# Tile stages in fewer bundles, memory sums with k and v side by side, final sums by pairs of experts, last weights in pieces

## The chip, the cores and the metric

The kernel runs on one core of one Trainium2 chip. The metric is the device time of one execution in microseconds (us); lower is better. The time before is the median of three runs.

## What is computed

Three layers in a row, cut from the reference; all data in fp32. x is first a memory attention over 4 batches of 576 tokens, then a mixture of 4 experts, then a soft mixture of 8 experts with 4 slots each.

```python
# attention: batch 4, heads 8, seq 576, head_dim 64, 32 memories
a = softmax(phi, over the sequence)
k_m = einsum('bhsm,bhsd->bhmd', a, k);  v_m = einsum('bhsm,bhsd->bhmd', a, v)
attn_out = softmax(q @ k_m.T / 8) @ v_m            # 2304 tokens x 512
# first mixture: 4 experts, D = 512, F = 1024
p = domain_probs / domain_probs.sum(-1)
out += p[:, e] * (relu(x @ w1[e]) @ w2[e])          # for e in 0..3
# second mixture: 8 experts, 4 slots each
logits = x @ phi2
slot_input = softmax(logits, over the tokens).T @ x
slot_out[e] = relu(slot_input[e] @ w1[e]) @ w2[e]   # v1, v2 in the kernel
out = softmax(logits, over the slots) @ slot_out
```

## The kernel before

The tokens run in five units: batches 0 to 2 whole (576 tokens), batch 3 as two halves of 288. The second mixture's input is never formed. `up` computes hidden values of the first mixture for 128 hidden units and up to 288 tokens: a **bundle** of six fp32r passes 128x288 (L767 to L769) over the attention weights A and the product g of w1 with v's memory (`g_mult`, L692, one w1 block of 1 MB each, copied out by ACT L701 and DVE L703). ACT takes the relu (L776), DVE transposes in 32x32 blocks (L782), POOL multiplies by p (L786); the result h stays for the slot sums. `logits` (L805, L812) multiplies the relu by M = w2 phi2, summed over hidden units in one PSUM bank.

M comes from `m_chunk`, eight chunks of 1 MB of w2: four whole-array transposes per chunk in four stages (**flips**, L836), copied by ACT or DVE (L842), then `part` (L854, 128x32 tiles, N = 128) and one more flip (L865). The batch's attention needs `memory`: flips `tops` (L465) and `back` (L480) for the maximum of phi, exp on ACT (L493), then the sums of k and v with the exp in four `whole` stages (L511, L516; 128x32 tiles, 64 columns), k first, v later; `total` (L530, L534) sums the exp; two flips `turn` (L554). `query` flips q (L600) and scores it (L612) five times a batch.

When a unit ends, `group` gathers its logits (L914, L919, L923) in a bank, ACT copies it to lr (L927), DVE transposes it to lc (L934), ACT takes the exp (L948), DVE transposes to dt (L954), and PE sums exp times h into four banks by `sums` (L972): 32x32 tiles, the row by the token block's quarter, the column by 2 x (block mod 2) + pair of experts. DVE adds them to srun (L992). After the last unit come the end stages: `turn_s` (L1201), w2 blocks (L1232), `slots` (L1246), v1 blocks (W1, L1275), flips (L1289), v2 blocks (W2, L1319) in 128x16 tiles, the fold of four tiles' rows into one (L1340), and the output (L1358), sent by SP and, for the last 64 tokens of each batch, by POOL (L365). `warm` (L1067) is a transpose of the identity that only keeps PE busy. R[0] to R[4] are places in SBUF; a weight block of the end goes to a place as soon as its last reader is through.

What sets the order: every stage is added with a due time `at`, a cost and keys that it reads and writes. `Plan.order` runs through time at build and gives each engine the ready stage with the smallest due time. For PE it keeps two classes: bundles (lag None) and all others. Among bundles another stage has to be due a LAG of 1 before the next bundle; outside, a bundle has to be due AHEAD of 8 before the others. TURN is the cost it puts on a change of class. `Uses` then settles which PSUM bank and SBUF place each use gets. m_at, a table of numbers, and base + offsets in `attention` set the due times.

```python
            gap = stages[a][0] - stages[b][0]
            return b if gap >= (stages[b][8] if tokens else -self.AHEAD) else a
```

Of the kernel before, what the change touches and what calls it, by code (L numbers as in the profile page):

```python
# [14 lines left out]
class Plan:  # L15
# [7 lines left out]

    HOP = 0.1
    RATE = 0.33
    LAG, AHEAD = 1, 8
# [40 lines left out]
    def order(self):  # L67
# [16 lines left out]
        def first(cand, t):  # L84
            cand = [n for n in cand if ready[n] <= t]
            a = min((n for n in cand if stages[n][8] is None), default=None)
            b = min((n for n in cand if stages[n][8] is not None), default=None)
            if a is None or b is None:
                return b if a is None else a
            gap = stages[a][0] - stages[b][0]  # L90
            return b if gap >= (stages[b][8] if tokens else -self.AHEAD) else a
        out = []
        while len(out) < len(stages):
# [57 lines left out]
class Uses:  # L151
# [7 lines left out]
    def __call__(self, *places, width=1):  # L159
        uid = len(self.kinds)  # L160
        self.kinds.append((places, width))
        return Use(self.found[uid] if self.found else places[0], uid)

    def settle(self, stages):
# [169 lines left out]
def program(  # L334
# [107 lines left out]
    def memory(b, at):  # L442
# [25 lines left out]
        add(PE, 0.4, tops, r=[("ph", 2), ("ph", 3), mxk, "cst"], w=[pk(b1)], at=at[1])  # L468
# [12 lines left out]
        add(PE, 0.4, back, r=[mbk, "cst"], w=[pk(b2)], at=at[2])  # L481
# [23 lines left out]
        def whole(w, c, t):  # L505
            rows = slice(64 * c, 64 * c + 64)
            for r_ in range(5):
                for i in range(4):
                    o = t[32 * i:32 * i + 32, 0:64]
# [11 lines left out]
        b3, b4 = att_bank(b), att_bank(b)  # L521
        for c, bk in enumerate((b3, b4)):
            add(PE, 0.85, lambda c=c, bk=bk: whole(0, c, bank[bk]),
                r=[("ph", c), ("ph", 2 + c), ("kt", 0, c), wk(o + 1024 * c, 1024)], w=[pk(bk)], at=at[4])
        t3 = bank[b4][:, 128:256]
# [9 lines left out]
        add(PE, 0.9, total, r=[smk, ("ph", 2), ("ph", 3), "cst"], w=[pk(b4)], at=at[4] + 0.1)  # L535
# [6 lines left out]
        def scaled(bks, dst, eng):  # L542
            for c in range(2):
                src = bank[bks[c]][:, 0:64]
# [20 lines left out]
        add(PE, 0.25, lambda: turned(km, kd, bank[b5], PE), r=[kmk, "cst"], w=[pk(b5)], at=at[5] + 0.1)  # L565
        add(DVE, 0.5, lambda: turned(km, kd, bank[b5], DVE), r=[pk(b5), "cst"], w=[("kb", b % 2)],
            at=at[5] + 0.2)
        b6 = [att_bank(b), att_bank(b)]
        for c in range(2):
            add(PE, 0.85, lambda c=c: whole(1, c, bank[b6[c]]),  # L570
                r=[("ph", c), ("ph", 2 + c), ("kt", 1, c), wk(o + 2048 + 1024 * c, 1024)], w=[pk(b6[c])],
                at=at[6])
        add(ACT, 0.65, lambda: scaled(b6, vm, ACT), r=[pk(b6[0]), pk(b6[1]), "rs"], w=[vmk], at=at[7])
        b7 = att_bank(b)
        add(PE, 0.25, lambda: turned(vm, vd, bank[b7], PE), r=[vmk, "cst"], w=[pk(b7)], at=at[8])
# [13 lines left out]
    def query(b, ti, at):  # L589
# [11 lines left out]
        add(PE, 0.42, flip, r=[qk, "cst"], w=[pk(b1)], at=at[0])  # L601
# [14 lines left out]
        add(PE, 0.5, score, r=[wk(qo, 512), ("kb", b % 2)], w=[pk(b2)], at=at[1])  # L616
# [62 lines left out]
    def g_mult(s, at):  # L679
# [7 lines left out]
        bs = [g_bank(), g_bank()]  # L687
# [61 lines left out]
    def up(u, n, fb, ki):  # L749
# [20 lines left out]
        add(PE, 0.81, f, r=[wk(go, 2048)] + a_part(b, 0, o0, w) + a_part(b, 1, o0, w), w=[pk(bm)], at=at, lag=None)  # L770
# [19 lines left out]
    def logits(u, n, at):  # L790
# [7 lines left out]
        def f():  # L798
# [11 lines left out]
            else:  # L810
                for m, ho in enumerate(hos):
                    nc.tensor.matmul(  # L812
                        lb[32 * (m % 4):32 * (m % 4) + 32, 0:HB], M[:, 4 * n0 + m, :], at_place(ho, HB),
# [3 lines left out]
        add(PE, 1.1, f,  # L817
            r=[("M", m) for m in range(n0, n + 1)] + [wk(o, width) for o in hos], w=[pk(LB)], at=at, lag=0)


    def m_chunk(n, ats):
# [9 lines left out]
        for a in range(4):  # L831
            bk = g_bank()
# [6 lines left out]
            add(PE, 0.42, flip, r=[wk(o + 512 * a, 512), "cst"], w=[pk(bk)], at=ats[1 + a])  # L839
# [9 lines left out]
        bk = g_bank()  # L849
# [583 lines left out]
```

## Time and profile before

| what | us |
|---|---|
| median of three runs (499.54 to 500.55) | 500.46 |
| the profiled execution | 503.48 |
| its span | 501.7 |
| PE busy | 472.7 |
| DVE busy | 297.4 |
| POOL busy | 214.7 |
| ACT busy | 199.7 |

Each matmul of fp32 appears as two passes in the trace, transposes and the fp32r bundles as one. Starts of passes lie closer together than they last, since passes overlap: the distance of two starts is what one costs, not its duration. The granted clock is the share of TensorE's 2.4 GHz that the chip gives in a stretch; 0.50 is 1.2 GHz. Idle time of an engine stands in brackets with what ended it.

### The profile page before, as it was taken

Reading aid. Unit: us, or ns where it says so; the run is one execution under the profiler, and the core shown is the slowest. Engines: PE = TensorE matmul, PEld = TensorE weight load, DVE = VectorE, ACT = ScalarE, POOL = GpSimd, SP = SyncE. Lnnn points to the kernel's source line nnn. Section 1 sums busy time; section 2 is a strip of 40 time slices with the busy share of each in tenths; the row PEclk is TensorE's granted clock in tenths of the full one; section 3 lists DMA queues with packets and bytes.
Section 4 is the critical chain, followed back from the end, with each engine's and each line's share of the span. In section 5 each row is a group of like instructions: output and inputs, shape, how many; then the busy total and the mean of one; then the engine's idle time right before and its main releaser. Section 6 shows DMA issues by size and latency. Waiting matters only on the chain.

```text
span 501.7 us, 13501 instructions
## 1 busy us (share of the span) xinstructions
PE 472.7 (94%) x5732; PEld 340.7 (68%) x5732; DVE 297.4 (59%) x606; ACT 199.7 (40%) x476; POOL 214.7 (43%) x259
## 2 busy tenths in 40 slices
PE   4899799999999999999999999999999989999991
PEld 2677688778876888788668887865797866333330
DVE  6589447676695867767684676676677544110041
ACT  2354245555551556555145555533552420011031
POOL 0244134557641448775224778533765940000001
PEclk9999899999999999999999999999999998789996
DMA  7999867425320946352082645524536997999928
GB/s 220 220 353 309 331 181 220 170 59 178 144 86 11 338 121 162 109 188 85 3 276 81 203 169 175 204 86 149 157 133 227 370 341 302 421 421 422 421 111 305
DMA packets 65404, 106.09 MB, mean 211 GB/s; under 512 B 28608, under 2 KB 40896, under 8 KB 59712
## 3 DMA queue, kind: packets, MB, share of 16 engines
q1 hardware_dynamic: 65152, 104.71, 61.3%
q8 instruction: 45, 0.74, 0.6%
q0 software_dynamic: 192, 0.52, 0.4%
q14 instruction: 15, 0.12, 0.1%
HBM read 100.50 MB, written 4.72 MB: 210 GB/s over the span
## 4 chain that ended last, share of the span: by engine, by line
PE 88%; DMA 4%; SPq 3%; DVE 1%; ACT 1%; issue 0%; DVEq 0%; ACTq 0%
PE ps L767 15%; PE ps L769 13%; PE ps L768 13%; PE ps L972 8%; PE ps L692 6%; PE ps L805 5%; PE ps L1275 4%; PE ps L836 3%; PE ps L1319 3%; SPq L365 3%; DMA raw<-in_moe_w_dram 3%; PE ps L1232 2%; PE ps L812 2%; DMA h<-in_moe_w_dram 2%; PE ps L854 2%; PE ps L600 2%
## 5 line engine op out<-in xcount | busy, mean ns | idle before, releaser
L786 POOL TENSOR_TENSOR h<-h,pe 128x576 f32<-128x576 f32 (+1 forms) x160 | 158.1, 996 | 137.6 <-DVE h L782 108.7
L767 PE MATMUL ps<-A,g 128*128 128x288 f32 x512 | 157.5, 308 | 0.0
L776 ACT ACTIVATE hts<-ps 128x288 f32<-128x288 f32 x256 | 105.2, 412 | 129.5 <-PE ps L769 128.1
L769 PE MATMUL ps<-A,g 128*128 128x288 f32 x512 | 151.5, 296 | 0.2 <-DVE g L703 0.2
L768 PE MATMUL ps<-A,g 128*128 128x288 f32 x512 | 151.2, 295 | 0.0
L782 DVE STREAM_TRANSPOSE h<-hts 128x576 f32<-128x576 f32 (+1 forms) x160 | 102.8, 648 | 46.9 <-ACT hts L776 46.5
L767 PEld LDWEIGHTS ps<-A,g 128*128 128x128 f32 x512 | 96.4, 188 | 21.5 <-issue 14.0
L769 PEld LDWEIGHTS ps<-A,g 128*128 128x128 f32 x512 | 96.2, 188 | 0.9 <-DVE g L703 0.9
L768 PEld LDWEIGHTS ps<-A,g 128*128 128x128 f32 x512 | 96.3, 188 | 0.1
L703 DVE TENSOR_TENSOR g<-ps,g 128x512 fp32r<-128x512 f32 x64 | 41.1, 680 | 17.8 <-ACT g L701 17.8
L701 ACT CAST g<-ps 128x512 fp32r<-128x512 f32 x64 | 34.9, 590 | 33.2 <-PE ps L692 33.2
L972 PE MATMUL ps<-h,dts 32*32 32x512 f32 x1152 | 40.0, 597 | 1.6 <-DVE dts L954 1.6
L365 POOL DMA_DIRECT2D out_dram<-v x4 | 2.3, 568 | 81.5 <-ACT v L1367 81.5
L692 PE MATMUL ps<-raw,vbs 64*32 64x512 f32 x512 | 35.2, 600 | 1.0 <-DMA raw<-in_moe_w_dram 1.0
L972 PEld LDWEIGHTS ps<-h,dts 32*32 32x32 f32 x1152 | 22.8, 103 | 15.2 <-issue 4.7
L805 PE MATMUL ps<-hts,M 128*32 128x288 f32 x384 | 28.2, 411 | 0.0
L629 POOL TENSOR_TENSOR atts<-atts,small 128x256 f32<-128x256 f32 (+1 forms) x20 | 11.5, 573 | 24.4 <-DVE small L627 24.3
L836 PE MATMUL ps<-ident,h 128*128 128x128 f32 x128 | 18.8, 286 | 2.8 <-DMA h<-in_moe_w_dram 2.8
L836 PEld LDWEIGHTS ps<-ident,h 128*128 128x128 f32 x128 | 15.1, 146 | 5.0 <-issue 3.6
L805 PEld LDWEIGHTS ps<-hts,M 128*32 128x32 f32 x384 | 10.4, 109 | 10.0 <-issue 4.5
L640 POOL TENSOR_TENSOR atts<-atts,small 128x256 f32<-128x256 f32 (+1 forms) x20 | 11.5, 573 | 13.4 <-DVE small L638 7.0
L842 DVE COPY h<-ps 128x512 f32<-128x512 f32 x16 | 10.8, 676 | 9.1 <-PE ps L836 9.0
(186 smaller groups left out, 519.7 us busy)
## 6 DMA issues: line engine op xcount, KB each, us to landing
raw<-in_moe_w_dram SPq DMA_DIRECT2D x32, 1024.0 KB, 5.2
v<-in_moe_w_dram SPq DMA_DIRECT2D x20, 1024.0 KB, 9.9
h<-in_moe_w_dram SPq DMA_DIRECT2D x18, 1024.0 KB, 9.0
h<-in_k_dram SPq DMA_DIRECT2D x8, 512.0 KB, 5.0
h<-in_v_dram SPq DMA_DIRECT2D x8, 512.0 KB, 6.5
atts<-in_moe_w_dram SPq DMA_DIRECT2D x4, 1024.0 KB, 8.1
atts<-in_q_dram SPq DMA_DIRECT2D x12, 256.0 KB, 5.8
atts<-in_phi_dram SPq DMA_DIRECT2D x8, 256.0 KB, 4.3
```

Of the source, the lines that this page charges most:

```text
L692: nc.tensor.matmul(bank[bs[c]][32 * i:32 * i + 32, :], vb[b % 2][64 * c:64 * c + 64, 32 * i:32 * i + 32], t()[64 * c:64 * c + 64, i, :], s ...
L701: add(ACT, act(512), lambda c=c, src=src: nc.scalar.copy(out=placed(g()[:, 2 * c]), in_=src), r=[pk(bs[c])], w=[wk(o + 1024 * c, 512)], at ...
L703: add(DVE, dve(512), lambda c=c, src=src: nc.vector.tensor_tensor(out=placed(g()[:, 2 * c + 1]), in0=src, in1=placed(g()[:, 2 * c].bitcast ...
L767: nc.tensor.matmul(t, gh, ah, start=(c == 0), stop=False)
L768: nc.tensor.matmul(t, gh, al, start=False, stop=False)
L769: nc.tensor.matmul(t, gl, ah, start=False, stop=(c == 1))
L776: add(ACT, act(w), lambda: nc.scalar.activation(out=t[:, o0 - base:o1 - base], in_=bank[bm][:, 0:w], func=ACTF.Relu,), r=[pk(bm)], w=[wk(h ...
L782: add(DVE, dve(width), lambda: nc.vector.transpose(out=h_of(u, e)[:, kx], in_=t), r=[wk(ho, width)], w=[hk], at=at + 0.4)
L786: add(POOL, pool(width), lambda: nc.gpsimd.tensor_tensor(out=h_of(u, e)[:, kx], in0=h_of(u, e)[:, kx], in1=share, op=ALU.mult), r=["pe"], ...
L805: nc.tensor.matmul(lb[r0:r0 + 32, 0:HB], M[:, 4 * n + a, :], at_place(hos[a] + o0, o1 - o0), start=(first and h == 0), stop=(not first and ...
L836: nc.tensor.transpose(bank[bk][:, 128 * c:128 * c + 128], wn()[:, a, 128 * c:128 * c + 128], ident)
L972: nc.tensor.matmul(bank[S0 + p][32 * c:32 * c + 32, :], dtv[rows, tb, :], h_pair(u, ep)[rows, :, :, tb, :], start=(tb < 2), stop=(tb >= nt ...
```

## The change

It has these parts.

1. Plan. Flips (whole-array transposes, and `total`) get a class of their own, WHOLE: they need no distance from the bundles, and go first when due up to EARLY = 2 behind the next bundle. Bundles are TOKENS. `part`, and `whole` and `score` of batches 1 to 3, keep a lag of 1.
2. `memory` of batches 1 to 3 sums k and v in the same stage: two stages of 128 columns instead of four of 64, and both results stay in two banks.
3. Flips and `part` of `m_chunk` take one of four banks instead of two, settled last (late); chunks come due in pairs; `attention` gets a table QUERY; `g_mult` of batch 3 comes due in pairs, with four banks.
4. `group`: DVE reads the bank before ACT. Nine warms instead of six before the last sums, and the very last sums run for experts' pair 0 over all token blocks, then for pair 1. The last logits stage is split 7 + 1.
5. End: two warms before `slots` and one behind; warms among the v2 blocks from expert 5 on instead of 4, and one instead of two for expert 7 (9 instead of 14). The last v2 block is loaded in three pieces (rows 0 and 1, 2, 3). Its fourth row-block doesn't go through the accumulator but straight into the fold's banks (`tail`), with a table hl that holds the slot's hidden values four times. The four outputs of a batch's last 64 tokens go through SP.

The diff, cut to its core:

```diff
+    LAG, AHEAD, EARLY = 1, 8, 2
+    WHOLE, TOKENS = None, -1
...
-            a = min((n for n in cand if stages[n][8] is None), default=None)
-            b = min((n for n in cand if stages[n][8] is not None), default=None)
+            a = min((n for n in cand if stages[n][8] == self.TOKENS), default=None)
+            w = min((n for n in cand if stages[n][8] is self.WHOLE), default=None)
+            if a is None or w is not None and stages[w][0] <= stages[a][0] + self.EARLY:
+                a = a if w is None else w
+            b = min((n for n in cand if stages[n][8] not in (self.WHOLE, self.TOKENS)), default=None)
...
-        def whole(w, c, t):
+        def whole(ws, c, t):
...
-                    o = t[32 * i:32 * i + 32, 0:64]
+                    o = t[32 * i:32 * i + 32, 0:64 * len(ws)].rearrange("p (w d) -> p w d", w=len(ws))
...
+        both = b > 0
         for c, bk in enumerate((b3, b4)):
+            ws = (0, 1) if both else (0,)
...
-            bk = g_bank()
+            bk = uses(S0, S0 + 1, S0 + 2, S0 + 3, late=True)
...
-            add(PE, 0.42, flip, r=[wk(o + 512 * a, 512), "cst"], w=[pk(bk)], at=ats[1 + a])
+            add(PE, 0.42, flip, r=[wk(o + 512 * a, 512), "cst"], w=[pk(bk)], at=ats[1 + a], lag=plan.WHOLE)
...
-        for ki, bk in enumerate((b1, b2)[:len(ranges)]):
-            add(ACT, act(HB), lambda ki=ki, bk=bk: nc.scalar.copy(
...
+        for ki, bk in enumerate((b1, b2)[:len(ranges)]):
+            add(ACT, act(HB), lambda ki=ki, bk=bk: nc.scalar.copy(
+                out=lr[:, HB * ki:HB * ki + HB], in_=bank[bk][:, 0:HB],
+            ), r=[pk(bk)], w=["lr"], at=at[0] + 0.2)
...
-        for t0 in range(0, nt, 2):
-            tbs = range(t0, min(t0 + 2, nt))
-            add(PE, 0.43 * len(tbs) + 0.02, lambda tbs=tbs: sums(tbs), r=["dt"] + hks, w=sb, at=at[3])
+        for eps in ((0,), (1,)) if final else ((0, 1),):
+            ks = [hks[e] for e in range(E) if e // 2 in eps]
+            for t0 in range(0, nt, 2):
+                tbs = range(t0, min(t0 + 2, nt))
+                add(PE, 0.43 * len(tbs) + 0.02, lambda tbs=tbs, eps=eps: sums(tbs, eps), r=["dt"] + ks, w=sb, at=at[3])
...
+            for a, z in ((0, 2), (2, 3), (3, 4)) if m == len(loads) - 1 else ((0, n),):
...
-    m_at = [2.5, 6.2, 10.5, 14.5, 18.5, 22.5, 26.5, 30.5]
+    m_at = [2.5, 6.2, 8.2, 14.2, 16.2, 22.2, 24.2, 30.2]
...
-                g_mult(s + 1, place(u, n, 1) + 0.1)
+                g_mult(s + 1, place(u, n if len(ranges) == 2 else n - n % 2, 1) + (0.1 if len(ranges) == 2 else 0.1 + 0.3 * (n % 2)))
...
-    warm(6, ["lr"], z4 + 2.6)
+    warm(9, ["lr"], z4 + 2.6)
...
+    warm(2, [pk(bw)], z + 1.95, (S0, S0 + 1))
...
     add(PE, 0.95, slots, r=[wk(PART, 512), "cst"], w=[pk(b1)], at=z + 2.1)
+    warm(1, [pk(b1)], z + 2.15, (S0, S0 + 1))
...
+            for kks in ((0, 1), (2,)) if last else (range(4),):
+                add(PE, 0.15 * len(kks), lambda kks=kks, f=f: f(kks),
+                    r=[tk[kk] for kk in kks] + [("hz", e // 2)], w=[pk(ab)], at=at + 0.001 * kks[0])
...
-            if 4 <= e and (e, nn) != (7, 1):
-                warm(2, [pk(ab)], at + 0.06, (S0, S0 + 1))
+            if 5 <= e and (e, nn) != (7, 1):
+                warm(1 if e == 7 else 2, [pk(ab)], at + 0.06, (S0, S0 + 1))
...
+            if n:
+                add(PE, 0.45, lambda h=h, cs=cs, t=t: nc.tensor.matmul(
+                    bank[bf[h]][:, 0:256], hl.rearrange("p c s -> p (c s)"), t(3)[:, cs], start=False, stop=False,
+                ), r=[tk[3], "pe"], w=[pk(bf[h])], at=at + 0.09 + 0.1 * h)
...
-                dma(
-                    out[b * S + 512:b * S + 576, :], lambda t=t, b=b, rows_out=rows_out: t()[rows_out, b // 2, :],
-                    131072, r=[k_], w=[wk(o + 512 * b, 512)], at=at + 0.05, cost=1.0, eng=POOL,
-                )
...
+                    for c in (b - 1, b):
+                        dma(
+                            out[c * S + 512:c * S + 576, :], lambda t=t, c=c: t()[64 * (c % 2):64 * (c % 2) + 64, c // 2, :],
+                            131072, r=[("tail", c)], w=[wk(o + 512 * c, 512)], at=at,
+                        )
```

Three places show how the instructions move. The lines of the changed kernel are higher by 9 to 40: bundles 778 to 780, flips of w2 850, `part` 868, its flip 879, g 703, `whole` 519 and 524, logits 816, warms 1088, W2 1352, `tail` 1377, fold 1380, output 1398.

The first is PE at the third w2 chunk, before: the last passes of the seventh bundle of the second g product, then the chunk's flips (L836) among `whole` (L511, L516) and `total` (L530) of batch 1.

```order
L769 MATMUL ps_92<-A,g 128x288
L836 MATMUL ps_96<-ident,h_103 128x128 x4
L836 MATMUL ps_97<-ident,h_103 128x128 x4
L511 MATMUL ps_98<-h_89,atts 32x64 x16
L516 MATMUL ps_98<-atts 32x64 x4
L836 MATMUL ps_96<-ident,h_103 128x128 x4
L836 MATMUL ps_97<-ident,h_103 128x128 x4
L511 MATMUL ps_99<-h_89,atts 32x64 x16
L516 MATMUL ps_99<-atts 32x64 x4
L530 MATMUL ps_99<-ind,atts 128x1
```

And now:

```order
L780 MATMUL ps_92<-A,g 128x288
L850 MATMUL ps_96<-ident,h_103 128x128 x4
L850 MATMUL ps_97<-ident,h_103 128x128 x4
L850 MATMUL ps_98<-ident,h_103 128x128 x4
L879 MATMUL ps_96<-ident,ct 128x128
L850 MATMUL ps_99<-ident,h_103 128x128 x4
L778 MATMUL ps_93<-A,g 128x288
```

The third chunk's flips still follow the same bundle; the last flip of the chunk before (L879) now stands among them, the third g product (L703) stands behind the bundle that begins here, and `whole` is gone from here.

The second is PE at the memory sums of batch 3, before: v's turn, after logits (L805).

```order
L554 MATMUL ps_98<-ident,atts 128x128
L805 MATMUL ps_95<-hts,M 32x288 x8
L511 MATMUL ps_99<-h_89,atts 32x64 x16
L516 MATMUL ps_99<-atts 32x64 x4
L511 MATMUL ps_98<-h_89,atts 32x64 x16
L516 MATMUL ps_98<-atts 32x64 x4
L692 MATMUL ps_96<-raw,vbs 32x512
```

And now, one of the two stages that hold k and v:

```order
L780 MATMUL ps_92<-A,g 128x288
L816 MATMUL ps_95<-hts,M 32x288 x8
L519 MATMUL ps_98<-h_89,atts 32x128 x16
L524 MATMUL ps_98<-atts 32x128 x4
L778 MATMUL ps_93<-A,g 128x288
```

The stage has 128 columns; its like, into bank 99, stands two bundles and a g product earlier, and nothing is left of v's own.

The third is PE at the last v2 blocks (L1319), warms (L1067) and fold (L1340), before:

```order
L1067 MATMUL ps_96<-ident 128x128 x2
L1067 MATMUL ps_97<-ident 128x128 x2
L1319 MATMUL ps_92<-h_89,vbs 16x512 x4
L1067 MATMUL ps_96<-ident 128x128 x2
L1067 MATMUL ps_97<-ident 128x128 x2
L1319 MATMUL ps_92<-h_89,vbs 16x512 x4
L1340 MATMUL ps_99<-lrs,r_69 128x256
L1340 MATMUL ps_98<-lrs,r_69 128x256
L1358 MATMUL ps_93<-kbs,ct 128x256
```

And now:

```order
L1088 MATMUL ps_97<-ident 128x128 x2
L1088 MATMUL ps_96<-ident 128x128 x2
L1352 MATMUL ps_92<-h_89,vbs 16x512 x4
L1088 MATMUL ps_97<-ident 128x128 x2
L1352 MATMUL ps_92<-h_89,vbs 16x512 x3
L1377 MATMUL ps_99<-h_89,pe 128x256
L1380 MATMUL ps_99<-lrs,r_69 128x256
L1377 MATMUL ps_98<-h_89,pe 128x256
L1380 MATMUL ps_98<-lrs,r_69 128x256
```

One warm stands ahead of the last block, which has three row-blocks instead of four; the fourth is in the two `tail` matmuls (L1377), one ahead of each half of the fold.

## Rows read from the trace of the kernel before

**Rows 1.** The page: busy time by engine; granted TensorE clock in 40 slices of the span.

```profile
PE 472.7 (94%) x5732; PEld 340.7 (68%) x5732; DVE 297.4 (59%) x606; ACT 199.7 (40%) x476; POOL 214.7 (43%) x259
...
PEclk9999899999999999999999999999999998789996
```

**Rows 2.** Busy time by stretch: us, PE (x), PEld, DVE, ACT, POOL, PEclk, DMA share, GB/s.

```profile
52.40:55.30 2.90, 0.17 (x2) 0.00 (x0) 0.96 (x2) 0.41 (x1) 1.61 (x2) 1.00 1.00 412
...
56.50:59.90 3.40, 3.40 (x64) 2.73 (x60) 0.94 (x2) 0.68 (x2) 0.00 (x0) 0.50 0.73 254
...
129.70:406.60 276.90, 276.42 (x3571) 213.67 (x3570) 191.73 (x362) 128.28 (x312) 158.95 (x188) 1.00 0.49 160
```

**Rows 3.** Chain of waits, 13 to 60: start us, us, what.

```profile
46.59 8.62 DMA h<-in_moe_w_dram
```

**Rows 4.** PE's timeline, the end: start us, us, engine, line, operation, tiles, count, [idle before].

```profile
411.61 5.38 PE L972 MATMUL ps<-h,dts 32*32 32x512 f32 x144 [1.60 <-DVE dts L954]
...
471.14 0.66 PE L1067 MATMUL ps<-ident 128*128 128x128 f32 x4
471.72 1.05 PE L1319 MATMUL ps<-v,h 128*16 128x512 f32 x8
...
482.68 1.16 PE L1340 MATMUL ps<-lrs,r 128*128 128x256 f32 x4 [0.49 <-ACT lrs L1334]
```

**Rows 5.** Busy time by stretch, the end.

```profile
421.80:428.60 6.80, 6.80 (x34) 2.97 (x37) 3.28 (x8) 0.44 (x1) 0.00 (x0) 0.50 1.01 420
435.40:442.20 6.80, 6.42 (x23) 1.75 (x26) 0.29 (x1) 0.00 (x0) 0.00 (x0) 0.50 1.03 422
470.10:479.90 9.80, 9.80 (x77) 3.43 (x80) 0.00 (x0) 0.00 (x0) 0.00 (x0) 1.00 0.81 332
479.90:482.10 2.20, 2.20 (x20) 0.55 (x12) 0.00 (x0) 0.00 (x0) 0.00 (x0) 1.00 0.00 0
```

**Rows 6.** PE's timeline, memory sums of a later batch.

```profile
256.92 0.65 PE L511 MATMUL ps<-h,atts 128*32 128x64 f32 x32 [0.28 <-ACT atts L493]
...
257.75 0.66 PE L511 MATMUL ps<-h,atts 128*32 128x64 f32 x32
```

**Rows 7.** PE's timeline, flips, bundles and part in the first batch.

```profile
78.75 0.60 PE L836 MATMUL ps<-ident,h 128*128 128x128 f32 x4
79.10 0.38 PE L767 MATMUL ps<-A,g 128*128 128x288 f32 x1
79.32 0.29 PE L768 MATMUL ps<-A,g 128*128 128x288 f32 x1
...
80.64 0.29 PE L769 MATMUL ps<-A,g 128*128 128x288 f32 x1
80.87 1.08 PE L854 MATMUL ps<-h,phi_sb 128*32 128x128 f32 x32
81.76 1.15 PE L805 MATMUL ps<-hts,M 128*32 128x288 f32 x16
```

**Rows 8.** Chain of waits, flips ahead of a tile stage.

```profile
277.90 0.59 PE ps L600 x4
278.49 1.02 PE ps L692 x16
```

**Rows 9.** The page: DMA issues, KB each, median us to landing.

```profile
raw<-in_moe_w_dram SPq DMA_DIRECT2D x32, 1024.0 KB, 5.2
```

**Rows 10.** Timelines of ACT and DVE, the last group.

```profile
408.73 0.40 ACT L927 COPY lrs<-ps 128x288 f32<-128x288 f32 x1 [3.17 <-PE ps L923]
...
409.16 0.48 DVE L934 STREAM_TRANSPOSE lcs<-ps 128x288 f32<-128x288 f32 x1 [1.27 <-ACT lrs L927]
```

**Rows 11.** Chain of waits, first W1 blocks and first half of W2.

```profile
436.34 11.77 PE ps L1275 x64
...
462.44 6.17 PE ps L1319 x56
```

**Rows 12.** The page: copies of flipped chunks (busy, mean ns | idle before, releaser).

```profile
L842 DVE COPY h<-ps 128x512 f32<-128x512 f32 x16 | 10.8, 676 | 9.1 <-PE ps L836 9.0
```

More of the change, by code (lines that the diff above doesn't have):

```diff
@@ L521, in memory @@
         b3, b4 = att_bank(b), att_bank(b)
+        both = b > 0
         for c, bk in enumerate((b3, b4)):
-            add(PE, 0.85, lambda c=c, bk=bk: whole(0, c, bank[bk]),
-                r=[("ph", c), ("ph", 2 + c), ("kt", 0, c), wk(o + 1024 * c, 1024)], w=[pk(bk)], at=at[4])
-        t3 = bank[b4][:, 128:256]
+            ws = (0, 1) if both else (0,)
+            add(PE, 1.2 if both else 0.85, lambda c=c, bk=bk, ws=ws: whole(ws, c, bank[bk]),
+                r=[("ph", c), ("ph", 2 + c)] + [("kt", w, c) for w in ws] + [wk(o + 2048 * w + 1024 * c, 1024) for w in ws],
+                w=[pk(bk)], at=at[4], lag=1 if b else plan.LAG)
+        t3 = bank[b4][:, 256:384]
         def total():
@@ L686, in g_mult @@
         t, tk = raw_of.pop(s)
-        bs = [g_bank(), g_bank()]
+        bs = [g_bank(), g_bank()] if b < B - 1 or n == 0 else [uses(S0, S0 + 1, S0 + 2, S0 + 3) for _ in range(2)]
         def f():
@@ L816, in logits @@
         width = ranges[-1][1] - base
-        add(PE, 1.1, f,
-            r=[("M", m) for m in range(n0, n + 1)] + [wk(o, width) for o in hos], w=[pk(LB)], at=at, lag=0)
+        last = u == NU - 1 and n == NCH - 1
+        for ms in (range(7), range(7, 8)) if last else (range(8),):
+            add(PE, 0.15 * len(ms) if last else 1.1, lambda ms=ms: f(ms),
+                r=[("M", m) for m in range(n0, n + 1)] + [wk(o, width) for o in (hos[ms[0]:ms[-1] + 1] if last else hos)],
+                w=[pk(LB)], at=at + (0.01 * ms[0] if last else 0), lag=0)
     def m_chunk(n, ats):
@@ L848, in m_chunk @@
                     r=[pk(bk)], w=[("wt", n % 2, a)], at=ats[1 + a] + 0.1)
-        bk = g_bank()
+        bk = uses(S0, S0 + 1, S0 + 2, S0 + 3, late=True)
         def part():
@@ L858, in m_chunk @@
         wtk = wk(o + 2048, 2048)
-        add(PE, 1.0, part, r=[("wt", n % 2, a) for a in range(4)] + [wtk, "phi2"], w=[pk(bk)], at=ats[5])
+        add(PE, 1.0, part, r=[("wt", n % 2, a) for a in range(4)] + [wtk, "phi2"], w=[pk(bk)], at=ats[5], lag=1)
         mp = ct[:, 0:128]
@@ L964, in group, with sums @@
         sb = [pk(n) for n in sbn]
-        def sums(tbs):
+        def sums(tbs, eps):
             for tb in tbs:
-                for ep in range(2):
+                for ep in eps:
                     c = 2 * (tb % 2) + ep
@@ L1302, in spread_h @@
                 )
-        add(DVE, 0.5, spread_h, r=[pk(bt)], w=[("hz", m)] + hzs[m][1], at=zz + 2.6)
+            if m == 3:
+                nc.vector.tensor_copy(
+                    out=hl[:, :, 28:32], in_=tv[:, 1, 1, 3, 28:32].unsqueeze(1).to_broadcast([128, 4, 4])
+                )
+        add(DVE, 0.6, spread_h, r=[pk(bt)], w=[("hz", m)] + hzs[m][1] + (["pe"] if m == 3 else []), at=zz + 2.6)
     so4 = kbs.rearrange("p n c x -> p (n c x)")
```

88 lines of the change are left out of this document (48 added, 40 removed).

## The prediction, made before the changed kernel had run

> **What bounds the kernel now.** I read the page's summary first, then the chain of waits, then PE's timeline and busy time by stretch. PE is busy for 472.7 us, 94% of the span [rows 1], and the last stretch of the body, 129.70 to 406.60, holds 276.42 us of PE work in 276.90 us [rows 2]. So in the body a microsecond of PE work taken away is a microsecond, as long as nothing else becomes late. Three places differ. At 52.40 to 55.30 PE does 0.17 us of work, because the third w2 chunk, issued at 46.59, lands 8.62 us later [rows 2, 3]; then the granted clock is 0.50 (1.2 of 2.4 GHz) from 56.50 to 59.90 [rows 2]. In the end, PE waits 1.60 for the group chain of DVE and ACT before the last sums [rows 4], and the clock is 0.50 twice more, 421.80 to 428.60 and 435.40 to 442.20 [rows 5]. From 470.10 on PE is busy without a gap, and since 479.90 no transfer runs [rows 5]: the last v2 block is there before PE wants it.
>
> The profiled execution took 503.48 us (span 501.7) against a median of 500.46: 3.0 us more. I work out differences on the trace and put them on the median.
>
> **The body: PE work.** (1) Memory sums. One `whole` stage of 64 columns takes 0.83 (256.92 to 257.75) [rows 6], so k and v of a batch take 4 x 0.83 = 3.32. Side by side there are 80 passes of 128 columns; 32 passes of that shape take 0.89 in `part` (80.87 to 81.76) [rows 7], hence 80 x 0.0278 = 2.23. That is -1.1 for each of batches 1 to 3: **-3.2**. (2) Turns. Four flips between two bundles take 0.35, and the next bundle's second pass comes 0.22 instead of 0.13 later [rows 7]; the same four flips ahead of a tile stage take 0.59 [rows 8], so a stay among tile stages costs 0.24, of which I give 0.2 to the way from flips to tiles and 0.05 to the way back. From a bundle to a tile stage it is 0.23 instead of 0.13 (80.64 to 80.87 [rows 7]), and some 0.07 at the return. By the order of the instructions, changes from flips to tiles fall from 23 to 13 (-2.0), from tiles to flips from 33 to 19 (-0.7), from bundles to tiles from 42 to 38 (-0.7), and those from bundles to flips rise from 18 to 27 (at 0.09: +0.8). That is -2.6; with each stage priced by its own neighbours -2.5, which I take (-2.0 to -2.8). Together PE has **5.7 us less** to do up to the last logits.
>
> The Trainium skill (TensorEngine Tiling (Array Packing), Key Properties) says that a change of tiling mode drains TensorE. By that flips among bundles, both on the whole array, would cost no turn, and (2) would be -3.4 instead of -2.6; the row at 79.32 has them at 0.09 each, and the sum goes by the row.
>
> **The body: what of it arrives.** Of the 5.7, 3.2 lie ahead of 129.70, the seventh logits stage. There the third chunk decides: the same bytes are queued ahead of it on SP, so it lands at 55.2 again. By the price of each stage, 2.2 us of the saving are made ahead of that landing, where they only lengthen the wait. 1.4 of these are no saving at all: one g product (1.02 [rows 8]), `back` and a `flipM` of about 0.4 ran ahead of the wait, and now stand behind it. So 1.1 remains behind the landing. PE now idles some 4.3 to 5 us instead of 2.9 [rows 2], and I expect the low clock to hold longer. In before it cost at most half of 3.40, 1.7; I add 0.8 (0 to 1.7). Net **-0.3** (-1.1 to +0.7). Later chunks find their home free 6 us and more ahead of need by the priced order, and 1 MB lands in 5.2 where the queue is not full (median of the raw loads [rows 9]), so I see no second such wait; the seventh chunk has the least to spare, about 1 us.
>
> Behind 129.70 the remaining **-2.5** (two batches' memory sums and a few turns; -2.0 to -2.8) should arrive whole, PE being the bound. Stalls: PE idles 0.48 us in that stretch [rows 2], 0.28 of it where `whole` waits for an exp [rows 6], and passes that overlap hide some tenths more. In after the sums stand later behind their exp, and the g products of batch 3 go in pairs well ahead of their bundles: **-0.5** (-0.9 to +0.2, since `total` and `turn` now stand closer). Body: -0.3 - 2.5 - 0.5 = **-3.3**.
>
> **The end.** (3) DVE takes the bank before ACT: the transpose at 409.16 waits for an ACT copy of 0.40 [rows 10]; the chain to the sums is on the path: **-0.4**. ACT's own copy gets later, but only the row softmax wants it. (4) Sums by pairs. All 16 tiles take 144 passes in 5.38 [rows 4]. A pair uses 8 tiles. The fullest of them has five matmuls, 10 passes; a pass of 512 columns takes 6.17 / 14 = 0.44 on its tile (56 passes on four tiles [rows 11]), so a half takes 4.4. The second half's tiles are free when the first half's last passes are issued, some 0.9 us before its end: 4.4 + 4.4 - 0.9 = 7.9, at a somewhat lower price of a pass 7.7: **+2.4**. Bounds: 0, as the passes are the same (fewer tiles can't be quicker), and 8.8 - 5.4 = +3.4. In return half of h is free 1.3 us earlier, so the last weights land earlier; worth nothing, as the row at 479.90 shows no transfer that PE waits for [rows 5]. (5) Of 14 warms among the last eight W2 blocks, 9 remain; a pair takes 0.58 (471.14 to 471.72) [rows 4], so 5 x 0.29 = **-1.5**. This holds as long as the blocks are there, and the last lands 2.2 us ahead of PE's end of W2. (6) The last block's fourth row-block goes through two passes of 256 columns for each half of the fold instead: one half lies in the 0.49 us that the fold waits for ACT's copy [rows 4], the other costs about 0.5, and W2 is shorter by 0.25: **+0.3**. (7) Three warms at `slots` stand in gaps where PE waits for ACT and DVE: nothing. Three more at the group lie in the gap before the sums: nothing. (8) The four tail outputs go through SP instead of POOL: SP has four issues more ahead of the last four, but the packets are those of the quicker queue: **0** (-0.8 to +0.8). End: -0.4 + 2.4 - 1.5 + 0.3 = **+0.8**.
>
> The Trainium skill (TensorE: Matmul & The Clock Gate, Part 3: Packing small matmuls) gives 10.6x for 16 tiles and 6.32x for nine. By that the sums would become 5.38 x 10.6 / 6.32 = 9.0, an estimate from that page, and (4) would be +3.6; the rows have 16 g passes on eight tiles in 1.02, which speaks for the smaller price.
>
> Sum: -3.3 + 0.8 = -2.5, that is 500.46 - 2.5 = **498.0**.
>
> **Rivals.** A is this forecast, 496.5 to 499.4 by its bounds. B: the warms at `slots` keep the clock up. The stretch 435.40 to 442.20 holds 6.42 us of PE work at 0.50 [rows 5]; of it 5.9 is W1 (from 436.34 [rows 11]), which would take half: -2.9, so **495.1**. For it: the stretch begins at the two gaps around `slots`, just where the warms go. Against it: in the stretch from 421.80 PE is busy for all of 6.80 us, and the clock is 0.50 none the less. The Trainium skill (TensorE: Matmul & The Clock Gate, Part 4: PE-mode transpose) says that transposes don't count as busy for the clock; the warms are transposes, and by that B gives nothing and the time stays with A. The trace doesn't settle it: with warms the clock is 1.00 from 470.10, but no row shows that part without them.
>
> C, slower: the flips' banks. In after, chunks 2 to 7 flip in rows of three to five stages, 0.43 apart, and each bank must be copied out by ACT or DVE (a DVE copy takes 0.676 [rows 12]) between the relu and transposes of the bundles. If `part` or the next flip waits one such copy in each of six chunks, that is 6 x 0.68 = +4.1: **502.1**. It decides from 3.6 us on. Against it: in before those copies wait for PE (9.1 us before them), not PE for them [rows 12], and four banks serve them now.
>
> D, no change: the front and the sums take the unfavourable ends, +0.7 at the chunk, -2.0 behind it, stalls 0, sums +3.4, the rest of the end -1.6: 501.0. Half of that way from A is 499.5; between the two lies **500.3**.
>
> **How the numbers follow.** A 0.43, B 0.28, D 0.15, C 0.14. A difference under 0.2% (1.0 us) is one that a measurement can hardly tell from none. Faster than 499.46: nearly all of A and B, 0.70; within 0.2%: D, 0.15; slower than 501.46: C with the worst of D, 0.15. The range goes from B's lower side, 494.3, to 500.9, which leaves out C and little else.
>
> **What would show it.** Body: `whole` of 128 columns at 1.1 a stage; the start of the last logits about 3.3 us earlier; PE idle for over 4 us before the third chunk, with a longer clock of 0.50 behind it. Sums of 7.7 us from first to last, starting 3.7 earlier than now, and DVE's transpose ahead of ACT's copy. W2's second half 1.5 us shorter at clock 1.00. B shows in the clock of the first W1 blocks. Wrong would be: PE waiting for ACT or DVE at flips or `part` in batch 0 (C), a clock of 0.50 among the last W2 blocks, or sums near 5.4 or 8.8.

## The result, and the profile after

The changed kernel takes 495.61 us (median of four runs, 494.29 to 496.63), the kernel before 500.50 beside it: ratio 0.990, 95% interval 0.988 to 0.992. That is 4.9 us less, twice the 2.5 that the prediction forecast, and inside its range. A second series gave 495.42 against 501.12 (0.989, 0.987 to 0.992).

First the page of the changed kernel: busy time by engine, and the granted clock in 40 slices.

```profile
PE 467.4 (95%) x5496; PEld 341.1 (69%) x5496; DVE 296.1 (60%) x607; ACT 199.1 (40%) x476; POOL 211.7 (43%) x256
...
PEclk9989999999999999999999999999999999999996
```


PE is busy for 5.3 us less than in [rows 1], but most of that is the clock: before's second trace, below, with as much time at half clock as this one ahead of the outputs, has 469.5, only 2.1 more. The page's slices show the clock without the dips of the end. Then the changed kernel's busy time by stretch (columns as in [rows 2]), at the third w2 chunk.

```profile
30.50:34.30 3.80, 3.71 (x23) 1.96 (x24) 2.60 (x9) 1.69 (x4) 1.79 (x3) 0.66 1.09 293
52.40:55.30 2.90, 2.85 (x22) 2.61 (x20) 1.27 (x3) 1.36 (x5) 2.25 (x2) 1.00 1.01 418
56.50:59.90 3.40, 3.40 (x41) 2.36 (x42) 2.03 (x4) 1.58 (x3) 0.54 (x1) 1.00 0.25 51
```

And the same view in the end.

```profile
420.00:427.10 7.10, 7.10 (x66) 2.07 (x66) 3.28 (x8) 0.44 (x1) 0.00 (x0) 1.00 1.01 422
430.20:436.00 5.80, 5.80 (x32) 1.59 (x36) 0.00 (x0) 0.00 (x0) 0.00 (x0) 0.71 1.03 427
454.40:472.30 17.90, 16.60 (x130) 5.42 (x128) 0.80 (x4) 0.37 (x1) 0.00 (x0) 1.00 1.01 412
472.30:477.30 5.00, 4.95 (x26) 1.98 (x26) 0.42 (x1) 0.74 (x2) 0.00 (x0) 1.00 0.09 32
```


PE works through 52.40 to 55.30, where it stood still in [rows 2], and the clock behind the chunk is 1.00; it is 0.66 earlier, at 30.50 to 34.30. In the end the loads run at 412 to 427 GB/s until 472.3, and only one stretch has a lower clock, 0.71 (0.50 from 431.1 to 434.5). The chain of waits of the changed kernel (start us, us, what) tells what that means.

```profile
401.21 1.23 PE ps L823 x16
...
406.79 7.40 PE ps L986 x144
414.18 2.04 DVE srun L1008 x5
...
435.99 18.32 DMA v<-in_moe_w_dram
454.37 17.93 DMA h<-in_moe_w_dram
472.35 1.05 PE ps L1352 x8
...
477.30 5.82 PE ps L1398 x38
```


The last logits begin at 401.21, 4.4 us earlier than the 405.60 of the first trace of before. But from 435.99 to 472.30 the chain of what ended last is two loads of 18 us each. A megabyte at 421 GB/s is 2.5 us, so each of them stood behind some six others in the queue. PE is off the chain, although [rows 5] show it busy there, and it waits for the last but one v2 block, in PE's timeline:

```profile
469.87 1.04 PE L1352 MATMUL ps<-h,vbs 128*16 128x512 f32 x4
470.83 0.66 PE L1088 MATMUL ps<-ident 128*128 128x128 f32 x4
472.35 1.05 PE L1352 MATMUL ps<-h,vbs 128*16 128x512 f32 x8 [0.86 <-DMA h<-in_moe_w_dram]
```


So the first thing to settle was whether the trace of before, with its unbroken work of PE in the end, shows what most of its executions are.

### The profile page after: what moved, and what is told of

The parts are those of the page before. It is cut to its first block, busy times and chain, and to the rows that moved or that the text cites. A ratio compares the mean times of both kernels' runs of the same rounds, so it can differ in the third digit from the quotient of the medians.

```text
span 494.2 us, 13047 instructions
## 1 busy us (share of the span) xinstructions
PE 467.4 (95%) x5496; PEld 341.1 (69%) x5496; DVE 296.1 (60%) x607; ACT 199.1 (40%) x476; POOL 211.7 (43%) x256
## 4 chain that ended last, share of the span: by engine, by line
PE 80%; DMA 13%; DVE 3%; SPq 1%; issue 1%; ACT 1%; DVEq 0%
PE ps L778 14%; PE ps L780 13%; PE ps L779 13%; PE ps L986 8%; PE ps L703 6%; DMA h<-in_moe_w_dram 6%; PE ps L816 5%; DMA v<-in_moe_w_dram 4%; PE ps L850 2%; PE ps L611 2%; DMA atts<-in_phi_dram 2%; PE ps L623 2%; PE ps L823 2%; DMA h<-in_q_dram 1%; SPq L371 1%; PE ps L1255 1%
## 5 line engine op out<-in xcount | busy, mean ns | idle before, releaser
L986 PE MATMUL ps<-h,dts 32*32 32x512 f32 x1152 | 42.0, 596 | 0.6 <-DVE dts L968 0.5
L703 PE MATMUL ps<-raw,vbs 64*32 64x512 f32 x512 | 36.6, 606 | 1.9 <-DVE g L714 1.9
L850 PE MATMUL ps<-ident,h 128*128 128x128 f32 x128 | 17.3, 278 | 0.8 <-DMA h<-in_moe_w_dram 0.8
L816 PEld LDWEIGHTS ps<-hts,M 128*32 128x32 f32 x384 | 11.5, 109 | 8.4 <-issue 3.5
L703 PEld LDWEIGHTS ps<-raw,vbs 64*32 64x32 f32 x512 | 6.5, 105 | 14.3 <-issue 9.6
L665 POOL TENSOR_TENSOR A<-atts,A 128x256 fp32r<-128x256 f32 (+1 forms) x20 | 13.5, 683 | 3.4 <-ACT A L663 3.1
```

Source lines behind the costliest of these rows:

```text
L703: nc.tensor.matmul(bank[bs[c]][32 * i:32 * i + 32, :], vb[b % 2][64 * c:64 * c + 64, 32 * i:32 * i + 32], t()[64 * c:64 * c + 64, i, :], s ...
L816: nc.tensor.matmul(lb[r0:r0 + 32, 0:HB], M[:, 4 * n + a, :], at_place(hos[a] + o0, o1 - o0), start=(first and h == 0), stop=(not first and ...
L850: nc.tensor.transpose(bank[bk][:, 128 * c:128 * c + 128], wn()[:, a, 128 * c:128 * c + 128], ident)
L986: nc.tensor.matmul(bank[S0 + p][32 * c:32 * c + 32, :], dtv[rows, tb, :], h_pair(u, ep)[rows, :, :, tb, :], start=(tb < 2), stop=(tb >= nt ...
```

## The experiments

The edits are against the changed kernel unless said otherwise. A time stands beside the before of its own series; intervals are some 0.5% wide, 2.5 us, so that where a difference is about 1 us the trace has to carry it. Edits are shown without their context.

**The kernel before, again** (no edit).

> The kernel before, unchanged, profiled and timed again. Theory 1: the two stretches of granted clock 0.50 in the end and the one behind the third w2 chunk stand in the first profiled execution (503.48) but not in most executions; in this profile at least one is missing, its mean clock is above 0.98, its own time is near 500.5, and the last v2 block lands some 62.7 us after the first of the end's loads is issued, with PE waiting for it. Theory 2: the stretches belong to the kernel; the clock is 0.975 again, and PE is busy without a gap at the last v2 blocks.

Measured: 500.71, with before at 500.87. The chain of waits of its profiled execution:

```profile
405.23 1.23 PE ps L812 x16
...
411.24 5.39 PE ps L972 x133
...
427.11 14.81 DMA v<-in_moe_w_dram
441.98 19.88 DMA v<-in_moe_w_dram
461.92 17.41 DMA h<-in_moe_w_dram
...
480.92 1.16 PE ps L1340 x4
482.08 5.82 PE ps L1358 x37
```


The clock was 1.00 behind the third chunk. It was half of full speed for one stretch of the end, 3.4 us where the first trace has two of 6.8, as the busy time by stretch shows:

```profile
432.40:435.80 3.40, 3.15 (x8) 0.73 (x10) 0.19 (x1) 0.00 (x0) 0.00 (x0) 0.53 0.98 401
```


Three loads are on the chain from 427.11 to 479.33. PE waits for v2 blocks (us in total, times, longest):

```profile
PE ps L1319 <- DMA h<-in_moe_w_dram: 1.7, 2, 0.9
...
PE ps L1319 <- DMA hts<-in_moe_w_dram: 0.3, 1, 0.3
```


That is theory 1: the loads bound the end of the kernel before, too. The expectation was missed in one point: this execution took 502.03, 1.3 above the median of its ten, and not about 500.5. Its mean clock was 0.984, and 12 of the 17 runs beside it had a higher one. With less time at half clock PE would come to the last blocks earlier still and wait longer, so most executions should be bound by the loads as well; no profile of one near the median shows it. In the first trace two stretches at half clock had put PE behind them: the last transfer ended by 479.90 [rows 5], and PE came to the last block at 481.13. In 17 runs of before the mean clock was between 0.975 and 0.992, and the two at 0.975 took 503.0 and 503.5 us, the longest of all. The first profiled execution, 503.48 at 0.975, was of that kind.

**The body alone** (before with the changed classes, memory sums, banks and due times; its end as it was).

> The changed body (plan classes, memory sums, chunk banks, due times) with the end of the kernel before. Theory 1: -2.9 us against before (497.6): -1.4 ahead of the seventh logits less the 1.5 that the low clock cost only in the first profile, and -3.0 behind it; the end, bound by its loads, moves along. Theory 2: -4.4 (496.1), the whole distance of the two traces at the last logits.

Measured: 497.92 against 500.87, -2.9; ratio 0.993 (0.991 to 0.995). Its last logits begin at 401.39. The ratio of all its runs is -3.6, with -2.5 to -4.7 allowed: the medians speak for theory 1's number, the ratio for neither. Behind the seventh logits the traces, compared below, give -2.8.

**The end alone** (the other half).

> The body of the kernel before with the changed end (DVE before ACT, sums by pairs, warms, pieces, tails through SP). Theory 1: -2.3 us (498.2): the end's first load is issued 1.4 us earlier against the last logits, and the outputs end 1.0 us earlier. Theory 2, PE bounds the end: sums +2.0, DVE first -0.4, warms -1.5, clock -2.9 with the warms at slots, outputs -1.0: -3.8 (496.7), or -0.9 where before has no low clock either.

Measured: 498.18 against 500.87, -2.7; ratio 0.994 (0.992 to 0.996). The two halves add up to 5.6 by the medians and 6.7 by the ratios (-3.1 for this one), the whole to 4.9 to 5.7: the same within the noise. The prediction had the end as a loss of 0.8. The chains divide it. From the last logits to the first output it is 76.85 us in the second trace of before and 76.99 with the new body alone, but 76.31 in this run and 76.09 in the changed kernel: -0.5 to -0.9. From the first output to the end of the span it is 18.1 and 18.0 against 16.8 and 16.9: -1.1 to -1.3. The next runs take both apart.

**The last sums in one pass.**

```diff
-        for eps in ((0,), (1,)) if final else ((0, 1),):
+        for eps in ((0, 1),):
```

> The changed kernel with the very last sums in one pass over both pairs of experts, as before. Theory 1 (the loads bound the end): half of h comes free 1.4 us later, the loads start later by that, and the time is 1.0 to 1.4 us above the changed kernel (496.8). Theory 2 (PE bounds the end): the sums take 5.4 instead of 7.4 us and the time is 2 us below it (493.6).

Measured: 496.13 against 500.87 (0.990): 0.5 to 0.7 above the changed kernel's two series, and nothing of theory 2's gain. PE's timeline of this run has the sums at their old length:

```profile
406.47 5.39 PE L986 MATMUL ps<-h,dts 32*32 32x512 f32 x144 [0.52 <-DVE dts L968]
```

Its chain of waits has the last logits and the last but one block:

```profile
400.89 1.23 PE ps L823 x16
...
472.49 1.05 PE ps L1352 x8
```


From the last logits to that block it is 71.60 here, 71.14 in the changed kernel and 71.07 in its copy: the sums by pairs cost PE 2.0 us (7.39 against 5.39) and bring the loads 0.46 forward. The times alone would not settle the sign, as 0.5 to 0.7 lies within their noise. It is less than the 1.4 expected, and busy time by stretch tells where the rest went: from 411 to 415 the loads run at 248 GB/s in the changed kernel and at 131 in this run, 0.47 MB or 1.1 us at 421 GB/s more; from 418 to 420 it is 332 against 418, 0.4 us less, since the longer sums put the w2 blocks and so the next loads off.

**Warms as before** (14 among the v2 blocks, none at `slots`).

```diff
-    warm(2, [pk(bw)], z + 1.95, (S0, S0 + 1))
-    warm(1, [pk(b1)], z + 2.15, (S0, S0 + 1))
-            if 5 <= e and (e, nn) != (7, 1):
-                warm(1 if e == 7 else 2, [pk(ab)], at + 0.06, (S0, S0 + 1))
+            if 4 <= e and (e, nn) != (7, 1):
+                warm(2, [pk(ab)], at + 0.06, (S0, S0 + 1))
```

> The changed kernel with 14 warms among the last v2 blocks and none at slots, as before. Theory 1, the loads bound the end: PE has 1.5 us more to do, of which it lacks 0.9 to 1.2 at the last blocks, so 0 to +0.6; a low clock at the first v1 blocks, if it comes, costs nothing, because PE waits for loads later on. Theory 2, PE bounds the end: +1.5 for the warms, and +2.9 more where the clock falls at slots.

Measured: 495.62 beside 495.42 for the changed kernel in the same series. 1.5 us of PE work more cost 0.2. And the clock held without the warms at `slots`, by this run's busy time by stretch, while the changed kernel's first trace has 0.50 from 431.1 to 434.5 with them:

```profile
426.00:430.00 4.00, 2.91 (x18) 2.08 (x12) 0.29 (x1) 0.59 (x1) 0.00 (x0) 1.00 1.00 412
430.00:436.00 6.00, 6.00 (x52) 1.90 (x52) 0.00 (x0) 0.69 (x1) 0.00 (x0) 1.00 1.02 421
436.00:442.00 6.00, 6.00 (x44) 1.99 (x40) 1.26 (x4) 0.69 (x1) 0.00 (x0) 1.00 1.02 426
```


**One load less.**

```diff
-            for a, z in ((0, 2), (2, 3), (3, 4)) if m == len(loads) - 1 else ((0, n),):
+            for a, z in ((0, 2), (2, 3), (3, 4)) if m == len(loads) - 1 else () if m == len(loads) - 2 else ((0, n),):
```

> The changed kernel without the load of the last but one v2 block (1 MB; the matmuls run on what lies in its place, so two row blocks of the result are wrong data). Theory 1, the loads bound the end: the last pieces land 2.5 us earlier and the time falls by 1.5 to 2.0, until PE's own work bounds. Theory 2, PE bounds the end: 0.

Measured: 493.70 beside 495.42, -1.7. Taking a megabyte away shortens the kernel, taking 2.0 us of PE's sums away didn't. In the chain of waits of this run the last load ends at 465.55, and from there on it is PE alone:

```profile
400.13 1.23 PE ps L823 x16
...
445.71 19.84 DMA hts<-in_moe_w_dram
...
467.23 1.95 PE ps L1352 x8
...
469.77 0.98 PE ps L1352 x8
...
471.12 0.97 PE ps L1352 x6
...
474.05 5.79 PE ps L1398 x37
```


From the last logits to the first output it is 73.92 here. In the unchanged copy of the changed kernel it is 75.99, by its chain:

```profile
400.60 1.23 PE ps L823 x16
...
454.20 17.43 DMA h<-in_moe_w_dram
...
476.59 5.82 PE ps L1398 x38
```


So PE has about 2 us to spare in the end: its waits for v2 blocks in that copy are 0.9, 0.9 and 0.2 us. That is what hides the longer sums or the old warms. In the first trace of the changed kernel, with its 3.4 us at half clock, they are 0.9 in all.

> The changed kernel, unchanged, as the measure for the three runs beside it. 495.6; the last v2 piece lands some 73.7 us after the last logits begin, and PE waits for it.

That copy measured 495.42, its chain again on the loads.

**The last block in one piece.**

```diff
-            for a, z in ((0, 2), (2, 3), (3, 4)) if m == len(loads) - 1 else ((0, n),):
+            for a, z in ((0, n),):
-                        stop=(e == 3 and nn == 1) or (e == 7 and nn == (0 if kk == 3 else 1)),
+                        stop=(e % 4 == 3 and nn == 1),
-            for kks in ((0, 1), (2,)) if last else (range(4),):
+            for kks in (range(4),):
...
```

(The two `tail` matmuls are out as well.)

> The changed kernel with the last v2 block loaded whole and its fourth row-block through the accumulator, as before. Theory 1, the loads bound the end: from the last landing to the end of the fold it takes 2.75 in a trace of before and 2.46 in the changed kernel, so +0.3. The prediction had the reverse, -0.3, with PE as the bound.

Measured: 496.32, ratio 0.991 (0.989 to 0.993), 0.9 above the copy in another series. The times don't resolve it. The chain has 76.34 us from the last logits (401.11) to the first output (477.45), 0.3 more than the 75.99 and 76.09 of the changed kernel's two traces: theory 1's sign and size.

**Tails through POOL** (the output hunk of the diff undone).

> The changed kernel with the four outputs of 64 tokens sent by POOL again. Theory 1: the outputs after the fold take 16.9 us in the changed kernel's trace and 17.9 to 18.1 in two traces of before, and this is POOL's queue: +1.0 to +1.2. Theory 2, as the prediction had it: what SP gains in packets it loses in four more issues, 0.

Measured: 496.71 beside 495.42: +1.3. Busy time by stretch in this run, from the last copies to the end:

```profile
483.20:494.10 10.90, 0.00 (x0) 0.00 (x0) 0.29 (x1) 0.07 (x1) 0.00 (x0) 0.59 0.78 269
```

And in the copy with SP:

```profile
483.80:493.50 9.70, 0.00 (x0) 0.00 (x0) 0.48 (x1) 0.25 (x1) 0.00 (x0) 0.58 0.83 307
```


The rest of the outputs moves at 269 GB/s with POOL and at 307 with SP, as means up to the end of the span. From the fold to the end of the span it is 18.3 against 16.9 us. It was 17.9 in the first trace of before. In the last 20 us POOL's queue took 8.0% of the DMA engines' time for 0.52 MB and SP's 37.3% for 4.19 MB, 1.7 times as much for a megabyte. That this is what slows the others is likely, but no run shows it by itself.

**Tails in pairs.**

```diff
-                    for c in (b - 1, b):
-                        dma(
-                            out[c * S + 512:c * S + 576, :], lambda t=t, c=c: t()[64 * (c % 2):64 * (c % 2) + 64, c // 2, :],
-                            131072, r=[("tail", c)], w=[wk(o + 512 * c, 512)], at=at,
-                        )
+                    dma(
+                        out.rearrange("(b s) d -> b s d", s=S)[b - 1:b + 1, 512:576, :],
+                        lambda t=t, b=b: t()[:, b // 2, :],
+                        262144, r=[("tail", b - 1), ("tail", b)], w=[wk(o + 512 * (b - 1), 1024)], at=at,
+                    )
```

> The changed kernel with the outputs of 64 tokens of two batches in one transfer of 256 KB: two issues on SP instead of four. In the changed kernel's trace SP issues the four from 483.61 to 486.30 and the last four outputs behind them, though their copies end by 484.5. If SP's issues hold the last outputs up, they go 1.3 us earlier and the time falls by 0.5 to 1.0; if the DMA rate bounds the outputs, 0.

Measured: 505.66, ten us slower. It told nothing about SP's issues, but something about transfers. The view of the DMA queues of this run gives the rate over the last 25 us in 40 slices:

```profile
GB/s 0 197 390 252 400 406 393 419 361 380 170 7 13 82 374 354 92 52 52 308 354 361 367 360 380 347 131 52 52 56 52 52 52 52 52 52 52 20 0 0
```


In most of the last slices the core moves 52 GB/s, an eighth of 421. The destination's outer dimension is 2.

**Tails last.**

```diff
-    for bs, rs in (..., (None, None), ((0, 1), (2, 3)), ((2, 3), (2, 3))):
+    for bs, rs in (..., ((0, 1), (2, 3)), ((2, 3), (2, 3)), (None, None)):
```

> The changed kernel with the outputs of 64 tokens computed, copied and sent last instead of ahead of the last four outputs. If SP's issues (0.65 us for each of the four) hold the last four outputs of 512 KB up, these go 2.6 us earlier and the end is four short transfers: -1 to -2.5. If the rate of the transfers bounds the outputs, the sum of bytes is the same and the time stays within 0.5.

Measured: 495.89, ratio 0.989 (0.987 to 0.992), that of the changed kernel, and 16.8 us from the fold to the end of the span against 16.9. SP's four issues hold nothing up.

**k and v apart** (`both = False`, the due times of `memory` as before).

> The changed kernel with k and v of every batch summed in stages of their own, 64 columns each, at the due times of before; all else as changed. By the prices of stages (0.83 for 64 columns, 1.1 for 128) batches 2 and 3 get 2.2 us of PE work more, and batch 1 1.1, which may hide at the third chunk: +2.2 to +3.3 if PE bounds the body. Rival, the body is bound by something else or the stages fill waits: under +1.

Measured: 496.64, ratio 0.993 (0.991 to 0.995): +1.2 by the medians, +1.7 by the ratios; expected 2.2 to 3.3. PE's timeline of one stage of batch 3 in the changed kernel tells part of why:

```profile
258.38 1.06 PE L519 MATMUL ps<-h,atts 128*32 128x128 f32 x32
259.36 0.42 PE L524 MATMUL ps<-atts 64*32 64x128 f32 x8
259.71 0.41 PE L778 MATMUL ps<-A,g 128*128 128x288 f32 x1
```


It takes 1.33 where 1.1 was forecast; the last eight passes, on 64 rows, take 0.35.

**Flips tied to the bundles.**

```diff
-    WHOLE, TOKENS = None, -1
+    WHOLE, TOKENS = 1.0, -1
-            w = min((n for n in cand if stages[n][8] is self.WHOLE), default=None)
+            w = None
-            b = min((n for n in cand if stages[n][8] not in (self.WHOLE, self.TOKENS)), default=None)
+            b = min((n for n in cand if stages[n][8] != self.TOKENS), default=None)
-                whole = lag in (self.WHOLE, self.TOKENS)
+                whole = lag == self.TOKENS
```

> The changed kernel with flips, total and warms treated like the tile stages again (a lag of 1 to the bundles), all due times as changed. By the order, changes from flips to tiles rise by 6 (1.2 us) and from tiles to flips by 6 (0.3), those between bundles and flips fall by 18 (-1.6): 0, within 0.5. Rival, the prediction's prices of turns are off and bundles among flips are nearly free: +1.0 or more.

Measured: 499.19, ratio 0.998 (0.996 to 0.999): 3.8 us above the copy, nearly all of the body's gain gone. PE's waits in it, as above:

```profile
PE ps L850 <- DMA h<-in_moe_w_dram: 2.3, 1, 2.3
...
PE ps L703 <- DMA raw<-in_moe_w_dram: 1.0, 1, 1.0
```

And in the changed kernel:

```profile
PE ps L703 <- DVE g L714: 1.9, 1, 1.9
...
PE ps L850 <- DMA h<-in_moe_w_dram: 0.8, 1, 0.8
```


**The same with the old due times.**

```diff
-    m_at = [2.5, 6.2, 8.2, 14.2, 16.2, 22.2, 24.2, 30.2]
+    m_at = [2.5, 6.2, 10.5, 14.5, 18.5, 22.5, 26.5, 30.5]
...
```

> Flips tied to the bundles as in the run before (3.7 us above the changed kernel), and the due times of w2's chunks and of the queries as in the kernel before; side by side sums and banks as changed. If those 3.7 come from due times that fit free flips only (waits for the third chunk, raw loads and q), this gives back 1 to 2.5 of them: 496.7 to 498.2. If they are the turns between bundles and tile stages, it stays at 499.2 or rises.

Measured: 498.38, ratio 0.995 (0.992 to 0.997): 0.8 to 1.3 us below the run with the new times, and 2.8 to 3.0 above the changed kernel. A fifth to a third of the loss would be due times that fit free flips only, but the intervals of the two runs overlap. The rest stays with tied flips.

The traces settle more than the times here. From the seventh to the last logits, which holds the memory sums of batches 2 and 3, PE hardly waits and the clock is 1.00. Busy time of this stretch in before's second trace, the changed kernel, k and v apart, and this last run:

```profile
129.33:405.16 275.83, 275.36 (x3555) 213.18 (x3554) 191.27 (x361) 128.40 (x312) 158.26 (x187) 1.00 0.48 159
128.28:401.14 272.86, 272.82 (x3396) 212.61 (x3395) 190.99 (x361) 127.78 (x312) 156.97 (x186) 1.00 0.49 160
128.75:402.29 273.54, 273.50 (x3555) 213.63 (x3555) 191.03 (x361) 128.03 (x312) 156.72 (x186) 1.00 0.48 160
128.93:403.33 274.40, 274.21 (x3379) 211.95 (x3378) 192.23 (x363) 128.14 (x313) 157.25 (x187) 1.00 0.48 159
```


It lasts 275.83 us in all three traces of the old body (two of before, one of the end alone) and 272.86 to 273.08 in the changed kernel, its copy and the body alone, so that differences of some tenths count. Tied flips make it 275.80, with the old due times 274.40; k and v apart cost 0.5 to 0.7. Ahead of this stretch the same body varies by 2.2 us between executions: the seventh logits begin at 129.70, 129.33 and 127.48 in the old one.

## Why the prediction was right or wrong

**The base.** "From 470.10 on PE is busy without a gap, and since 479.90 no transfer runs": true of the first trace, wrong as a bound. That execution was 3.0 us above the median, which the prediction noted; it worked out differences on that trace and "put them on the median", as if the 3.0 were spread evenly. The second profiled execution of before shows that the loads bound the end. This is the step that failed, and the terms of the end fall with it: the prediction's +0.8 from PE's work measured -0.5 to -0.9 up to the first output, where PE waits 2.0 us for v2 blocks that the prediction had ready, and -1.1 to -1.3 behind it, in the outputs.

**(1) Memory sums, -3.2.** The direction holds, the size was too large. A stage takes 1.33, so a batch gives 3.32 - 2.66 = 0.7 rather than 1.1, and the two batches behind the seventh logits 1.3 rather than 2.2. The trace of k and v apart has 0.5 to 0.7 there; the whole of it, 1.2 to 1.7 by the times, is no better known than to about a microsecond.

**(2) Turns, -2.5.** Too small behind the seventh logits, where the prediction had 0.3 of it. Free flips and the due times that go with them give 1.3 to 1.5 there by the traces. The count of turns (9 changes more from tiles to flips, 2 from flips to tiles, 5 from bundles to tiles, but 11 fewer from bundles to flips) gives 0.5 + 0.4 + 0.9 - 1.0 = 0.7 by the prediction's prices. What in the prices is off was not measured by itself. For the whole body it is 2.8 to 3.0 by the times, with 1 to 4.5 allowed, too wide to check a price.

**The third chunk, -0.3.** The seventh logits begin 1.4 us earlier than in the first trace (PE's timeline of the changed kernel):

```profile
128.28 1.18 PE L816 MATMUL ps<-hts,M 128*32 128x288 f32 x16
```


No long wait and no low clock came: PE waits 0.8 us for the chunk. The likely reason is that its first bundles had begun late, 32.64 against 29.30, and at a clock of 0.66; PE's idle time moved forward, where it waits 1.9 for g on DVE. But before's second trace has the clock at 1.00 there as well, and 0.50 from 29.6 to 33.0 like the changed kernel, and the seventh logits begin anywhere from 127.48 to 129.70 in the old body, so what the change itself gives at this place stays open. Behind it, from the seventh to the last logits, it is 272.86 against 275.83: -3.0 as forecast. That is luck in part, the sum of a term too large and one too small.

**(3) DVE first, -0.4.** Right: the sums begin 5.58 behind the last logits, 6.01 before. It also brings the loads behind the sums forward: SP issues the first of them 11.11 us behind the last logits with the sums in one pass, 11.54 in the second trace of before. What of that reaches the last block was not measured by itself.

**(4) Sums by pairs, +2.4.** PE's price was nearly right, 7.39 against 5.38. That it would lengthen the kernel was wrong, and "worth nothing" of the earlier loads was wrong: they are what counts, 0.46 us by the traces. By the speedups in the Trainium skill (TensorE: Matmul & The Clock Gate, Part 3: Packing small matmuls) the estimate was 9.0; the measured 7.39 decides for the smaller price.

**(5) Fewer warms, -1.5.** 0.2: hidden by the loads. **(6) The last block in pieces, +0.3.** By the traces it is -0.3: its sign was wrong, for the same reason, as what counts is the time from the last landing on. **(7) Warms in gaps, nothing.** Right. **(8) Tails through SP, 0 (-0.8 to +0.8).** -1.3, outside the bounds: with POOL's packets the phase of outputs was slower, 269 against 307 GB/s.

**The rivals.** B's 495.1 is close to what was measured, but its mechanism is not it: without the warms at `slots` the clock was 1.00 there, with them it was 0.50 for 3.4 us in one trace and 1.00 in the copy's, and 1.5 us of PE work cost 0.2. The rule on transposes and the clock was not tested by this. C did not come: PE's waits show no ACT or DVE copy of a flipped chunk. D's ends were not reached.

As a sum over the median: body -2.9 (forecast -3.3), end -2.7 by itself and -2.0 beside the new body (forecast +0.8). So the miss lies in the end; in the body only the sum was right.

## What to carry to other kernels

A profiled execution that lies well above the median of the runs may show another bound than most runs have: profile it a second time before its waits are priced, or price each term against both bounds. Where loads run without a break up to the end, ask of each edit what it does to their start and their rate; PE work is then free up to PE's waits for the last loads, here 2.0 us in one execution and 0.9 in another. Outputs were bound by their rate here, so the queue that sent them counted more than the number of issues. And where times can't tell two edits apart, look for a stretch whose length is the same in every trace of one kernel, and compare there.

## What the runs showed of the hardware

A transfer of 2 x 64 x 512 elements from 128 partitions ran at 52 GB/s, where four of 64 x 512 ran in a phase at 307. The Trainium skill (DMA: Bandwidth & Descriptors, Why a DMA increments its semaphore by 16 and not by 1) says that a transfer is spread over the largest number of engines, up to 16, that divides the slowest dimension of both its sides. For a destination of 2 that is two, and an estimate from it is an eighth of 421 GB/s, 53; the trace agrees.

The same kernel's executions differ in where the clock is 0.50: before's first trace has it behind the third chunk and twice in the end, its second has 1.00 behind the chunk and one shorter stretch in the end, 3.4 us, and 17 runs had mean clocks from 0.975 to 0.992. Only a part of that reaches the time: the two runs at 0.975 had lost 8.5 us more of full clock than the three at 0.992, and took 2.6 us more.
